# Seven half-size products for eight in the second batch's first feed-forward matmuls

## Chip, cores and metric

One NeuronCore of a Trainium2 chip. The metric is the device time of one execution in microseconds (us), the median of three runs.

## What is computed

Three stages for B = 2 batches of S = 768 tokens, model width 512: attention within clusters (8 heads of 64), then a feed-forward layer with hidden width 2048, then a mixture of 4 experts with hidden width 1024 each. In float32, shortened:

```python
def _moe_ref(x, w_in, w_out):            # x: 1536 x 512
    h = x @ w_in                         # 512 x 2048
    relu6 = np.clip(h + 3.0, 0.0, 6.0)
    g = h * relu6 / 6.0
    return g @ w_out                     # 2048 x 512

def _moe2_ref(x, domain_probs, w1, w2):  # w1: 4 x 512 x 1024
    p = domain_probs / (domain_probs.sum(-1, keepdims=True) + 1e-09)
    out = 0
    for e in range(4):
        h = np.maximum(x @ w1[e], 0.0)
        out += p[:, e:e + 1] * (h @ w2[e])
    return out
```

## The kernel before

**Number format.** Each operand of a matmul stands as a high part (a copy rounded to the matmul's float32 format) and a low part (the rest). A product of two tiles is three matmuls into the same PSUM bank: high by high, high by low, low by high (`mm3`, L784 to L793). For a weight tile of 128x512, `split_w` (L747 to L751) makes the high part on ScalarE (ACT, L749) and the low part on GpSimd (POOL, L750); the latter reads both the raw tile and the high part.

**Stages.** Both batches run attention (`Attn`), then `Moe1` (the feed-forward layer, L797) and `Moe2` (the experts, L846). The attention of batch 1 is planned under `Moe2` of batch 0, so that `Moe1` and `Moe2` of batch 1 come last and alone. The hidden width is cut into chunks c of 512 columns: 4 in `Moe1`, 8 in `Moe2`. The tokens are cut into 2 blocks (blk) of MB = 384. A chunk's weights are 4 tiles k (128 rows each) of w_in or w1 in pool `wi` and 4 of w_out or w2 in pool `wo`. Each pool has 4 places, so that a chunk's weights go into the places of the chunk before.

**First matmul** (`g1`). For each block and each f (4 groups of 128 hidden columns), 12 matmuls of 128x384 (4 tiles k, 3 matmuls each) into one PSUM bank. In `Moe1` then ACT makes t (L820), VectorE (DVE) multiplies t by the bank (L821), ACT copies the high part of g (L822), DVE makes its low part g (L826). In `Moe2` ACT makes the high part of h (L864), DVE the low part (L865).

**Second matmul** (`g2`). In `Moe1` for each block and each of 4 groups d of output columns, 12 matmuls of 128x384, added by DVE to acc (L839; for c = 0 ACT copies, L837). Once c = 3 is added, ACT and DVE make x2h and x2l (L842, L843), the input of `Moe2`. In `Moe2`, for each block and each of 3 groups of 128 tokens, 12 matmuls of 128x512 with h as the stationary operand, scaled and added to oa by DVE (L880; L878 for c = 0), which is stored at the last chunk (L884). g2 of one block is planned among g1 of the next one. `psg`, `psm` in the profile are the PSUM banks of `Moe1` and `Moe2`; the pool `ps_mb` behind them has 3.

**Order.** The whole program is recorded first. `Order.plan` then takes, engine by engine, the instruction that a model of the engines would start earliest; ties go to the lower priority number, which is a planned time (the loop over `seq`). The model's durations are formulas in `act`, `dve`, `pool`, `mm`. Loads of weights all go through SP's queue.

```python
def dve(n, prio, fn, r, w, fast=False, ap=False):
    return add("DVE", 1e-3 * (n / (1.92 if fast else 0.96) + 68 + 60 * ap), prio, fn, r, w)
def pool(n, prio, fn, r, w, ns=2.1):
    return add("POOL", 1e-3 * (n * ns + 150), prio, fn, r, w)
mm = lambda n: 1e-3 * (n / 2.4 + 2.5)
```

Of the kernel before, what the change touches and what calls it, by code (L numbers as in the profile page):

```python
# [99 lines left out]
class Buf:  # L100
    """A tile that its first writer allocates."""
# [230 lines left out]
def body(ctx: ExitStack, tc: tile.TileContext, qk, nat, vd, cent, w_in, w_out, probs, w1, w2, out):  # L332
# [48 lines left out]
    g_ps = o.group("psum", after=(g_pa,), keep=True)  # L381
# [18 lines left out]
    p_pm = [Pool("ps_ma", 1, g_pa, True), Pool("ps_mb", 3, g_ps, True)]  # L400
# [3 lines left out]
    p_acc = [Pool(f"acc{b}", 1, g_m[b]) for b in range(B)]  # L404
# [65 lines left out]
    class Attn:  # L470
# [76 lines left out]
            # scores against the centroids: rows (half of the tokens, head, q or k, centroid)  # L547
# [104 lines left out]
        def block(self, hp, blk, p, kinds, xb, avp):  # L652
            """A block of queries of a pair of heads; p(i) is the priority of its i-th unit."""
# [46 lines left out]
        def scores(self, qa, qb, ka, kb, q0, tb, n, p):  # L700
# [44 lines left out]
    wt, wscr = {}, {}  # L745
# [51 lines left out]
    class Moe1:  # L797
# [7 lines left out]
        def load(self, c, n, p):  # L805
# [40 lines left out]
    class Moe2:  # L846
# [64 lines left out]
    seq = [(st, c, blk) for st in stages for c in range(st.nch) for blk in range(NMB)]  # L911
# [4 lines left out]
    for st, c, blk in seq:  # L916
# [3 lines left out]
        tail = [(prev, d) for d in range(prev[0].n2)] if prev else []  # L920
# [6 lines left out]

        cut = len(tail) - 1 if blk == 0 else 0
# [83 lines left out]
```

## Time and profile before

| | |
|---|---|
| median of 3 runs | 1090.08 us (1089.95 to 1092.23) |
| span of the profiled execution, first to last instruction | 1088.1 us |
| PE (TensorE) matmul busy | 995.6 us, 91% |
| DVE / ACT / POOL busy | 634.4 / 478.7 / 497.8 us |
| granted TensorE clock, mean | 0.965 |
| PE in 850 to 1050 us | 50.00 of every 50 us |
| DVE in the same stretches | 13.25 to 13.64 of 50 us |

The profiled execution's own time is known as its span; the runs' times hold what lies around it too. The page's slices show the program in three parts: up to some 300 us attention and the conversion of weights for batch 0 with the other engines as busy as PE, then `Moe2` of batch 0 with the attention of batch 1, and from some 680 us on the two feed-forward stages of batch 1. Matmul spans overlap (a matmul of 0.33 us starts 0.17 us after the one before), so the cost of a matmul is read from starts, not from spans.

### The profile page before, as it was taken

What the parts mean: (1) busy time and instruction counts of PE and PEld (TensorE: products, weight loads), DVE (VectorE), ACT (ScalarE), POOL (GpSimd) and SP (SyncE); (2) the same over time, 40 slices, a digit from 0 to 9 for tenths busy, and PEclk for the clock granted to TensorE, in tenths of its full rate; (3) what the DMA queues carried; (4) which work ended last, traced back from release to release, by engine and by line L of the source; (5) the groups of instructions that cost most, each with busy time, mean ns of one, the idle gap of its engine ahead of it and who ended that gap; (6) DMA issues with size and microseconds to landing.
All of it is one profiled execution on the core that took longest, in us unless ns stands there. A gap on an engine that the chain in (4) does not pass through costs nothing.

```text
span 1088.1 us, 15473 instructions
## 1 busy us (share of the span) xinstructions
PE 995.6 (91%) x5699; PEld 898.5 (83%) x5699; DVE 634.4 (58%) x1103; ACT 478.7 (44%) x893; POOL 497.8 (46%) x385
## 2 busy tenths in 40 slices
PE   3666677988999999999999999999999999999998
PEld 1555556887898888888898898999999899999997
DVE  8999995999536785576476475334453222222222
ACT  6667774545255554345345343444342232222220
POOL 3576864546346776356256164234332333132330
PEclk9678888999999999999999999999999999999999
DMA  8599799676006486367266176222121221112211
GB/s 259 128 201 184 140 187 242 223 245 200 30 2 208 125 168 148 94 134 162 80 145 137 44 156 155 77 78 79 41 67 48 78 78 64 53 50 69 78 39 58
DMA packets 192363, 129.32 MB, mean 119 GB/s; under 512 B 155488, under 2 KB 155488, under 8 KB 192288
## 3 DMA queue, kind: packets, MB, share of 16 engines
q1 hardware_dynamic: 192288, 128.34, 46.1%
q8 instruction: 44, 0.72, 0.3%
q14 instruction: 31, 0.25, 0.1%
HBM read 74.51 MB, written 11.53 MB: 79 GB/s over the span
## 4 chain that ended last, share of the span: by engine, by line
PE 45%; DVE 18%; issue 16%; DMA 9%; POOL 8%; ACT 3%; SPq 1%; POOLq 0%; ACTq 0%; DVEq 0%
PE psm L789 12%; PE psm L791 12%; PE psm L790 12%; DMA pt<-p 6%; POOL w L750 4%; DVE p L741 4%; DVE ut L717 2%; PE psg L790 2%; DVE wconv L773 2%; DVE wconv L770 2%; PE psv L686 2%; PE psg L789 2%; PE psg L791 2%; DVE wconv L775 1%; POOL p L734 1%
## 5 line engine op out<-in xcount | busy, mean ns | idle before, releaser
L750 POOL TENSOR_TENSOR w<-wraw,w 128x512 fp32r<-128x512 f32 x160 | 213.6, 1365 | 289.7 <-ACT w L749 283.6
L864 ACT ACTIVATE h<-psm 128x384 fp32r<-128x384 f32 x128 | 62.4, 488 | 254.9 <-PE psm L791 252.1
L789 PE MATMUL psm<-x2h,w 128*128 128x384 f32 x512 | 173.2, 338 | 0.0
L791 PE MATMUL psm<-x2h,w 128*128 128x384 f32 x512 | 171.8, 336 | 0.0
L790 PE MATMUL psm<-x2l,w 128*128 128x384 f32 x512 | 171.5, 335 | 0.0
L865 DVE SCALAR_TENSOR_TENSOR h<-psm,h 128x384 fp32r<-128x384 f32 x128 | 71.0, 555 | 144.9 <-ACT h L864 144.7
L789 PE MATMUL psm<-w,h 128*128 128x512 f32 x384 | 151.5, 395 | 0.4 <-DVE h L865 0.4
L791 PE MATMUL psm<-w,h 128*128 128x512 f32 x384 | 150.8, 393 | 0.0
L790 PE MATMUL psm<-w,h 128*128 128x512 f32 x384 | 150.4, 392 | 0.0
L880 DVE SCALAR_TENSOR_TENSOR oa<-psm,pr,oa 128x512 f32<-128x512 f32 x84 | 62.8, 748 | 100.8 <-PE psm L791 100.8
L718 ACT ACTIVATE e<-pss,ut 128x768 f32<-128x768 f32 x96 | 86.0, 897 | 72.4 <-DVE ut L717 50.3
L789 PEld LDWEIGHTS psm<-x2h,w 128*128 128x128 f32 x512 | 96.1, 188 | 4.1 <-issue 2.4
L749 ACT ACTIVATE w<-wraw 128x512 fp32r<-128x512 f32 x160 | 93.7, 624 | 11.8 <-PE psm L791 8.1
L741 DVE SCALAR_TENSOR_TENSOR p<-e,ut,p 128x768 f16<-128x768 f32 x62 | 87.6, 1420 | 17.5 <-POOL p L739 15.7
L790 PEld LDWEIGHTS psm<-x2l,w 128*128 128x128 f32 x512 | 96.2, 188 | 1.3
L791 PEld LDWEIGHTS psm<-x2h,w 128*128 128x128 f32 x512 | 96.1, 188 | 0.0
L790 PE MATMUL psg<-g,w 128*128 128x384 f32 x256 | 88.9, 347 | 6.2 <-DVE g L826 4.4
L789 PE MATMUL psg<-x1h,w 128*128 128x384 f32 x256 | 87.3, 341 | 7.7 <-DVE t L821 7.6
L717 DVE TENSOR_REDUCE ut<-pss 128x1 f32<-128x768 f32 x96 | 90.0, 944 | 4.6 <-PE pss L712 4.5
L789 PE MATMUL psg<-g,w 128*128 128x384 f32 x256 | 87.9, 343 | 4.9 <-DVE t L821 4.5
L791 PE MATMUL psg<-g,w 128*128 128x384 f32 x256 | 87.4, 341 | 0.3 <-POOL w L750 0.3
L791 PE MATMUL psg<-x1h,w 128*128 128x384 f32 x256 | 86.7, 339 | 0.0
(125 smaller groups left out, 1913.4 us busy)
## 6 DMA issues: line engine op xcount, KB each, us to landing
wraw<-in_w SPq DMA_DIRECT2D x128, 256.0 KB, 3.2
r<-in_w_in SPq DMA_DIRECT2D x16, 512.0 KB, 5.0
r<-in_w_out SPq DMA_DIRECT2D x16, 512.0 KB, 4.4
nat<-in_nat SPq DMA_DIRECT2D x16, 384.0 KB, 4.4
raw<-in_qk SPq DMA_DIRECT2D x16, 384.0 KB, 4.2
scr_i<-wconv SPq DMA_DIRECT2D x16, 256.0 KB, 2.4
scr_o<-wconv SPq DMA_DIRECT2D x16, 256.0 KB, 3.2
wraw<-scr_i SPq DMA_DIRECT2D x16, 256.0 KB, 2.6
```

The lines of the kernel that those rows point to most:

```text
L686: nc.tensor.matmul(ps[64 * q:64 * q + 64], vs[vi][:, q, t], pts[q][:, :, pi * NT + t], start=i == 0, stop=i == n - 1)
L717: dve(S, p, lambda: nc.vector.tensor_reduce(out=nb(), in_=ps[:, :, 0:HS], axis=AX.XY, op=ALU.max, negate=True), [ps], [(tb, n)])
L718: act(S, p, lambda: nc.scalar.activation(out=e.t.rearrange("p (a b) -> p a b", a=2), in_=ps[:, :, 0:HS], func=AF.Exp, bias=nb(), scale=1.0 ...
L741: dve(S, p, lambda: nc.vector.scalar_tensor_tensor(out=pp[:, j, 1], in0=e.t, scalar=rs(), in1=pp[:, j, 0], op0=ALU.mult, op1=ALU.subtract) ...
L749: act(512, p, lambda: nc.scalar.activation(out=w[:, 0], in_=raw.t, func=AF.Copy), [raw], [(w, 0)])
L750: pool(512, p, lambda: nc.gpsimd.tensor_tensor(out=w[:, 1], in0=raw.t, in1=w[:, 0].bitcast(F32), op=ALU.subtract), [raw, (w, 0)], [(w, 1)])
L789: nc.tensor.matmul(o_, ah, bh, start=i == 0, stop=False)
L790: nc.tensor.matmul(o_, ah, bl, start=False, stop=False)
L791: nc.tensor.matmul(o_, al, bh, start=False, stop=i == 3)
L864: act(MB, p, lambda: nc.scalar.activation(out=h[:, 0], in_=ps[:, 0:MB], func=AF.Relu), [ps], [(h, 0)], ps=True)
L865: dve(MB, p, lambda: nc.vector.scalar_tensor_tensor(out=h[:, 1], in0=ps[:, 0:MB], scalar=0.0, in1=h[:, 0].bitcast(F32), op0=ALU.max, op1=A ...
L880: dve(512, p, lambda: nc.vector.scalar_tensor_tensor(out=oa[:, t], in0=ps.t, scalar=q, in1=oa[:, t], op0=ALU.mult, op1=ALU.add), [ps, pr], ...
```

## The change

For batch 1, in every chunk but c = 0 of each stage, the first matmul is computed as a whole: W (512 x 512) and X (512 x 768) are cut into quarters (two row halves of 256, two column halves), and the product's four quarters come from 7 products of quarters or sums of quarters instead of 8 (Strassen's identity, in Winograd's form).

- `sums_x`, once a stage: four sums of quarters of x (tiles tx0 to tx3, high and low). In `Moe1` they are built from x1h and x1l (28 DVE instructions of 128x384 and 8 ACT ones), in `Moe2` in place in acc (16 and 8).
- `load_w(..., sums=True)`: after the split of the raw weight tiles, four sums of quarters in place in the raw tiles (8 DVE instructions of 128x256), then their high parts on ACT (4) and low parts on DVE (4 of 128x512), into tiles ws.
- `g1w`, for each half i of the columns: 7 products of 6 matmuls each, every one into a bank of the new pool `ps_w` (5 banks). An ACT copy (u1) and 7 DVE adds put them together, partly in PSUM, partly in SBUF tiles "keep". `post` is what followed the matmuls in `g1`.
- Memory: `ps_w` opens when the attention's banks close; acc of batch 1 takes the place of oa; block 1's g and h get a pool `gw` of 5.
- Plan: both blocks of such a chunk are one step; the second matmuls of the chunk before are placed ahead of it and between the products of the second half.

The core of the diff (line numbers of the new kernel differ from those above; removed comments are left out):

```diff
-    p_acc = [Pool(f"acc{b}", 1, g_m[b]) for b in range(B)]
+    p_acc = [Pool("acc0", 1, g_m[0]), p_oa]
+    p_w = Pool("ps_w", 5, g_pf, True)
+    p_tx = Pool("tx", 8, g_m[1])
+    p_ws = Pool("ws", 8, g_m[1])
+    p_tmp = Pool("tmp", 6, g_m[1])
+    p_gw = Pool("gw", 5, g_m[1])
...
+        for k in range(2 if sums else 0):
+            u, v = raws[k], raws[k + 2]
+            a11, a21, a12, a22 = (lambda x=x, h=h: x[:, 256 * h:256 * h + 256] for x in (u, v) for h in range(2))
+            for o_, x, y, op, rd, w in ((a22, a21, a22, ALU.add, u, v), (a21, a11, a21, ALU.subtract, u, u), (a11, a22, a11, ALU.subtract, v, u), (a12, a12, a11, ALU.subtract, u, v)):
+                dve(256, p, lambda o_=o_, x=x, y=y, op=op: nc.vector.tensor_tensor(out=o_(), in0=x(), in1=y(), op=op), [rd] if rd is not w else [], [w])
+            for x in (u, v):
+                w = Buf(p_ws, [128, 2, 512], F32R, "ws")
+                act(512, p, lambda w=w, x=x: nc.scalar.activation(out=w[:, 0], in_=x.t, func=AF.Copy), [x], [(w, 0)])
...
+                    dve(512, p, lambda lo=lo: lo(nc.vector), [x, (w, 0)], [(w, 1)])
...
+            n = {1: (a(0, 0), bq(0, 0)), 2: (a(1, 0), bq(1, 0)), 3: (sm(2), bq(1, 1)), 4: (a(1, 1), tq(3)),
+                 5: (sm(3), tq(0)), 6: (sm(0), tq(1)), 7: (sm(1), tq(2))}
...
+            def kept(ps, k, j):
+                o = Buf(p_tmp, [128, MB], F32, "keep")
+                if k is None:
+                    act(MB, ts[j], lambda: nc.scalar.activation(out=o.t, in_=ps[:, 0:MB], func=AF.Copy), [ps], [o], ps=True)
+                else:
+                    dve(MB, ts[j], lambda: nc.vector.tensor_tensor(out=o.t, in0=ps[:, 0:MB], in1=k.t, op=ALU.add), [ps, k], [o])
+                return o
+
+            def done(blk, f, ps, k, j):
+                dve(MB, ts[j], lambda: nc.vector.tensor_tensor(out=ps[:, 0:MB], in0=ps[:, 0:MB], in1=k.t, op=ALU.add), [k], [ps])
+                self.post(c, blk, f, ps, lambda: ps[:, 0:MB], ts[j])
+
+            u1 = kept(prod(1), None, 1)
+            done(0, i, prod(2), u1, 2)
+            u2 = kept(prod(6), u1, 6)
+            u3 = kept(prod(7), u2, 7)
+            done(0, i + 2, prod(4), u3, 4)
+            p5 = prod(5)
+            o5 = kept(p5, u2, 5)
+            o4 = kept(p5, u3, 5)
+            self.post(c, 1, i + 2, o4, lambda: o4.t, ts[5])
+            done(1, i, prod(3), o5, 3)
...
+        wino = lambda self, c: self.b == 1 and c > 0
...
+            cut = len(tail) // 2 if prev[0].wino(prev[1]) else len(tail) - 1
+            t = second(tail[:cut], t)
+            for i in range(2):
+                ts = {}
+                for n, j in enumerate((1, 2, 6, 7, 4, 5, 3)):
+                    if i == 1 and n in (0, 2, 4):
+                        t = second(tail[cut + n // 2:cut + n // 2 + 1], t)
+                    ts[j] = t
+                    t += G3
+                if i == 1:
+                    t = second(tail[cut + 3:], t)
+                todo[st].append((st.g1w, (c, i, ts)))
```

**How the order moves.** DVE in `Moe1` of batch 1, around the first matmul of chunk 1. Before, t and the low half of g of one group after another (t, g: tiles of `post`; psg1: PSUM bank of a first product):

```order
L821 SCALAR_TENSOR_TENSOR t_7445<-t_7445,psg1_7427 128x384
L826 TENSOR_TENSOR g_7462<-t_7445,g_7462 128x384
L821 SCALAR_TENSOR_TENSOR t_7493<-t_7493,psg1_7464 128x384
L826 TENSOR_TENSOR g_7505<-t_7493,g_7505 128x384
L821 SCALAR_TENSOR_TENSOR t_7515<-t_7515,psg1_7487 128x384
L826 TENSOR_TENSOR g_7526<-t_7515,g_7526 128x384
```

With the change, the end of the same chunk's second half (psw: bank of a product; keep: a kept sum; wraw: raw tiles of the next chunk's w_in; ws: their sums' parts):

```order
L946 SCALAR_TENSOR_TENSOR t_7706<-t_7706,psw_7671 128x384
L775 TENSOR_TENSOR wraw_7570<-wraw_7570 128x256
L896 TENSOR_TENSOR keep_7726<-psw_7681,keep_7688 128x384
L775 TENSOR_TENSOR wraw_7570<-wraw_7610,wraw_7570 128x256
L775 TENSOR_TENSOR wraw_7633<-wraw_7595,wraw_7633 128x256
L775 TENSOR_TENSOR wraw_7610<-wraw_7610,wraw_7570 128x256
L775 TENSOR_TENSOR wraw_7595<-wraw_7595 128x256
L779 TENSOR_TENSOR ws_7742<-wraw_7570,ws_7742 128x512
L779 TENSOR_TENSOR ws_7750<-wraw_7610,ws_7750 128x512
L775 TENSOR_TENSOR wraw_7595<-wraw_7633,wraw_7595 128x256
L951 TENSOR_TENSOR g_7724<-t_7706,g_7724 128x384
```

Between t_7706 and its low half g_7724, which a second matmul reads, stand nine instructions, eight of them for the next chunk's weights.

PE between two chunks of `Moe1` of batch 1. Before, at the end of chunk 1's second matmuls (psg2: bank of a second product; w_7481 is w_out's last tile of chunk 1, w_7654 w_in's first of chunk 2):

```order
L789 MATMUL psg2_7745<-g_7693,w_7481 128x384
L790 MATMUL psg2_7745<-g_7693,w_7481 128x384
L791 MATMUL psg2_7745<-g_7693,w_7481 128x384
L789 MATMUL psg1_7768<-x1h1_4182,w_7654 128x384
L790 MATMUL psg1_7768<-x1l1_4188,w_7654 128x384
L791 MATMUL psg1_7768<-x1h1_4182,w_7654 128x384
```

With the change, at chunk 1's last second product (w_7584: w_out's last tile of chunk 1, w_8019: its first of chunk 2):

```order
L814 MATMUL psg2_8007<-g_7794,w_7584 128x384
L815 MATMUL psg2_8007<-g_7794,w_7584 128x384
L816 MATMUL psg2_8007<-g_7794,w_7584 128x384
L814 MATMUL psg2_8037<-g_7859,w_8019 128x384
L815 MATMUL psg2_8037<-g_7859,w_8019 128x384
L816 MATMUL psg2_8037<-g_7859,w_8019 128x384
```

The first products that stood between the second products of two chunks are gone from there; chunk 2's second product follows chunk 1's at once.

## Rows read from the trace of the kernel before

**Rows 1.** Busy time by stretch, all engines: 250 to 300 us, Moe1 chunks, one Moe2 chunk.
```profile
core 0: us, PE busy (x) PEld busy (x) DVE busy (x) ACT busy (x) POOL busy (x), PEclk, DMA share, GB/s
250.00:300.00 50.00, 43.37 (x229) 40.45 (x228) 36.36 (x53) 17.61 (x33) 23.75 (x18) 0.97 0.28 93
707.00:741.00 34.00, 33.54 (x193) 33.12 (x192) 12.92 (x20) 14.57 (x29) 10.93 (x9) 1.00 0.22 63
775.00:809.00 34.00, 33.54 (x194) 33.12 (x193) 18.09 (x28) 14.79 (x29) 11.04 (x8) 1.00 0.20 63
809.00:843.00 34.00, 33.54 (x182) 31.68 (x182) 13.90 (x22) 11.27 (x24) 11.04 (x8) 1.00 0.20 62
909.00:942.00 33.00, 33.00 (x169) 30.07 (x168) 8.80 (x15) 8.39 (x17) 10.11 (x8) 1.00 0.20 64
```

**Rows 2.** Timeline of PE: matmul starts in Moe1, then Moe2 (start us, us, what).
```profile
701.74 0.33 PE L789 MATMUL psg<-x1h,w 128*128 128x384 f32 x1
...
707.29 0.33 PE L791 MATMUL psg<-x1h,w 128*128 128x384 f32 x1
...
884.41 0.39 PE L789 MATMUL psm<-w,h 128*128 128x512 f32 x1
...
887.17 0.33 PE L789 MATMUL psm<-x2h,w 128*128 128x384 f32 x1
...
895.52 0.39 PE L789 MATMUL psm<-w,h 128*128 128x512 f32 x1
```

**Rows 3.** Waits, 690 to 1088 us: total us, times, longest.
```profile
PE psg L790 <- DVE g L826: 1.8, 4, 0.5
```

**Rows 4.** Groups by line, 700 to 1088 us (busy us, mean ns, idle before).
```profile
L750 POOL TENSOR_TENSOR w<-wraw,w 128x512 fp32r<-128x512 f32 x88 | 114.9, 1340 | 254.7 <-ACT w L749 254.7
...
L865 DVE SCALAR_TENSOR_TENSOR h<-psm,h 128x384 fp32r<-128x384 f32 x64 | 35.7, 558 | 103.9 <-ACT h L864 103.9
L880 DVE SCALAR_TENSOR_TENSOR oa<-psm,pr,oa 128x512 f32<-128x512 f32 x42 | 31.5, 751 | 76.7 <-PE psm L791 76.7
L826 DVE TENSOR_TENSOR g<-t,g 128x384 fp32r<-128x384 f32 x27 | 24.3, 901 | 17.2 <-ACT g L822 17.2
...
L821 DVE SCALAR_TENSOR_TENSOR t<-t,psg 128x384 f32<-128x384 f32 x27 | 14.9, 551 | 31.3 <-ACT t L820 31.3
...
L839 DVE TENSOR_TENSOR acc<-acc,psg 128x384 f32<-128x384 f32 x24 | 13.2, 553 | 17.9 <-PE psg L791 17.9
```

**Rows 5.** Groups by line of VectorE, whole execution.
```profile
L449 DVE TENSOR_TENSOR cw<-cn 128x64 f32<-128x64 f32 x1 | 0.2, 225 | 0.2 <-DMA cn<-in_cent 0.2
```

**Rows 6.** The line of g's low half: min/median/max ns.
```profile
L826 DVE TENSOR_TENSOR g<-t,g x40: 544/559/1692, 193.2 to 812.0; 128x384 fp32r<-128x384 f32 x40
```

**Rows 7.** Timelines of ScalarE, GpSimd and VectorE at a reload of w2.
```profile
918.51 2.70 ACT L749 ACTIVATE w<-wraw 128x512 fp32r<-128x512 f32 x4 [0.26 <-PE psm L791]
...
919.22 5.05 POOL L750 TENSOR_TENSOR w<-wraw,w 128x512 fp32r<-128x512 f32 x4 [4.79 <-ACT w L749]
...
920.53 0.75 DVE L880 SCALAR_TENSOR_TENSOR oa<-psm,pr,oa 128x512 f32<-128x512 f32 x1 [1.68 <-PE psm L791]
```

**Rows 8.** Timeline of VectorE, then of GpSimd, around a split of weights.
```profile
708.49 0.54 DVE L821 SCALAR_TENSOR_TENSOR t<-t,psg 128x384 f32<-128x384 f32 x1
709.79 1.59 DVE L826 TENSOR_TENSOR g<-t,g 128x384 fp32r<-128x384 f32 x1 [0.76 <-ACT g L822]
...
706.86 5.66 POOL L750 TENSOR_TENSOR w<-wraw,w 128x512 fp32r<-128x512 f32 x4 [19.54 <-ACT w L749]
```

**Rows 9.** Timeline of VectorE: last x1l, and t of chunk 0's second block.
```profile
683.68 0.48 DVE L696 SCALAR_TENSOR_TENSOR x1l<-psv,sv,x1h 128x256 fp32r<-128x256 f32 x1 [0.89 <-ACT x1h L694]
...
704.17 0.55 DVE L821 SCALAR_TENSOR_TENSOR t<-t,psg 128x384 f32<-128x384 f32 x1 [8.70 <-ACT t L820]
```

**Rows 10.** DMA issues (KB each, us to landing), whole execution.
```profile
wraw<-in_w SPq DMA_DIRECT2D x128, 256.0 KB, 3.2
```

**Rows 11.** The page's first line.
```profile
span 1088.1 us, 15473 instructions
```

More of the change, by code (lines that the diff above doesn't have):

```diff
@@ L380, in body @@
     g_pa = o.group("psum")
-    g_ps = o.group("psum", after=(g_pa,), keep=True)
+    g_pm = o.group("psum", after=(g_pa,), keep=True)
+    g_ps = o.group("psum", after=(g_pa,))
+    g_pf = o.group("psum", after=(g_ps,), keep=True)
     g_m[0] = o.group("left", after=(g_a[0], g_l0))
@@ L751, in split_w, with load_w @@
         wt.setdefault(key, []).append(w)
-    def load_w(key, src, p):
+    def load_w(key, src, p, sums=False):
+        raws = []
         for k in range(4):
@@ L798, in body @@
+    class Moe1(Wino):
         names, nch, n2 = "io", NC1, 4
@@ L809, in load @@
             else:
-                load_w(key, lambda k: wscr[key[1:]][k], p)
+                load_w(key, lambda k: wscr[key[1:]][k], p, sums=n == "i" and self.wino(c))
+        wino = lambda self, c: self.b == 1 and c > 0
+        src = lambda self: list(x1[1])
+        xs = lambda self: x1[1]
         def g1(self, c, blk, f, p):
@@ L817, in g1, with post @@
                 lambda k: [ps, w[k]] + xkeys(b, k, blk), xkeys(b, KD - 1, blk) if (b, c, blk) == (0, 0, 0) else ())
+            self.post(c, blk, f, ps, lambda: ps[:, 0:MB], p)
+        def post(self, c, blk, f, ps, out, p):
+            b, sb = self.b, ps.pool is p_tmp
             t = Buf(p_t[b], [128, MB], F32, "t")
-            g = Buf(p_g, [128, 2, MB], F32R, "g")
-            act(MB, p, lambda: nc.scalar.activation(out=t.t, in_=ps[:, 0:MB], func=AF.Relu, scale=1.0 / 6.0, bias=half[:, 0:1]), [ps], [t], ps=True, ap=True)
-            dve(MB, p, lambda: nc.vector.scalar_tensor_tensor(out=t.t, in0=t.t, scalar=1.0, in1=ps[:, 0:MB], op0=ALU.min, op1=ALU.mult), [ps], [t])
+            g = Buf(p_gw if self.wino(c) and blk else p_g, [128, 2, MB], F32R, "g")
+            act(MB, p, lambda: nc.scalar.activation(out=t.t, in_=out(), func=AF.Relu, scale=1.0 / 6.0, bias=half[:, 0:1]), [ps], [t], ps=True, ap=True)
+            dve(MB, p, lambda: nc.vector.scalar_tensor_tensor(out=t.t, in0=t.t, scalar=1.0, in1=out(), op0=ALU.min, op1=ALU.mult), [ps], [t])
             act(MB, p, lambda: nc.scalar.activation(out=g[:, 0], in_=t.t, func=AF.Copy), [t], [(g, 0)])
@@ L854, in load @@
             src = {"1": w1, "2": w2}[n][c]
-            load_w((self.b, n, c), lambda k: src[:, k], p)
+            load_w((self.b, n, c), lambda k: src[:, k], p, sums=n == "1" and self.wino(c))
+        wino = lambda self, c: self.b == 1 and c > 0
+        src = lambda self: [stages[2].acc]
+        xs = lambda self: x2s[1]
         def g1(self, c, blk, f, p):
@@ L910, in body @@
         stages += [Moe1(b), Moe2(b)]
-    seq = [(st, c, blk) for st in stages for c in range(st.nch) for blk in range(NMB)]
+    seq = [(st, c, blk) for st in stages for c in range(st.nch) for blk in range(NMB) if not (st.wino(c) and blk)]
     prev = None
@@ L919, in body @@
         start.setdefault(st, t)
-        tail = [(prev, d) for d in range(prev[0].n2)] if prev else []
+        tail = [(prev[:2] + (k,), d) for k in ((0, 1) if prev[0].wino(prev[1]) else prev[2:]) for d in range(prev[0].n2)] if prev else []
         def second(x, t):
@@ L926, in second @@
             return t
+        if st.wino(c):
+            if c == 1:
+                todo[st].append((st.sums_x, (start[st] + G["wx"],)))
+            todo[st].append((st.load, (c, st.names[0], t - G["wl"])))
+            G3 = 1.04
+            cut = len(tail) // 2 if prev[0].wino(prev[1]) else len(tail) - 1
[10 more added lines that the diff above has]
+                todo[st].append((st.g1w, (c, i, ts)))
+                if i == 0:
+                    todo[st].append((st.load, (c, st.names[1], t - G["wl"])))
+            prev = (st, c, 0)
+            continue
         cut = len(tail) - 1 if blk == 0 else 0
@@ L941, in body @@
         prev = (st, c, blk)
-    for d in range(prev[0].n2):
-        todo[prev[0]].append((prev[0].g2, (*prev[1:], d, t)))
-        t += G2
+    for k in range(NMB) if prev[0].wino(prev[1]) else prev[2:]:
+        for d in range(prev[0].n2):
+            todo[prev[0]].append((prev[0].g2, (*prev[:2], k, d, t)[1:]))
+            t += G2
     def trace(st):
```

77 lines of the change are left out of this document (70 added, 7 removed).

## The prediction

> **What bounds the kernel now.** I read the views in this order: the busy times by stretch, to find what is full where the change works; the matmul starts, for the price of a matmul; the groups by line, for the price of everything else; the timelines of VectorE, GpSimd and ScalarE, for what collides. The first 4459 PE instructions (all of batch 0 and of the second batch's attention) stand in the same order in both programs, so only what follows the first chunk of the second batch's first feed-forward stage counts, about 690 us onward. There TensorE is full: 33.54 of 34 us in each of the four windows from 707 to 843, about a chunk each of the first stage (Moe1), and 33.00 of 33 in a chunk of the second (Moe2), at a granted clock of 1.00, the 2.4 GHz level [rows 1]. VectorE is at 12.92 to 18.09 us per chunk in Moe1 and only 8.80 in Moe2. So a matmul taken away is time taken away, as long as VectorE can carry what it is given for it. In Moe1 it has 16 us free in a chunk, in Moe2 24.
>
> **Removed.** A chunk's first matmul is 8 products of 12 matmuls; the change makes 14 half-size products of 6. That is 84 for 96, in 3 chunks of Moe1 and 7 of Moe2: 120 fewer, and PE's list is shorter by just these 120, so the change does what it says. Matmuls of 384 columns start 5.55 us apart over 32 steps in Moe1 and 8.35 us over 48 in Moe2 [rows 2]: 0.1735 us each. **-20.8 us**, 2.08 per chunk. The waits of today, 0.46 us in each of the four windows (the waits view gives 1.8 us of matmuls to the low half of g), stand at places that are rebuilt: **-1.8** [rows 1, 3].
>
> **Added on VectorE, per chunk.** 14 adds of a product in PSUM to a kept sum, 128x384: like the acc add, 0.553 us, 7.7 us [rows 4]. For the weights, 8 sums of 128x256 and 4 low halves of 128x512, both operands in SBUF. No row has these shapes with two SBUF operands: 128x64 takes 0.225 [rows 5] and 128x384 0.559 when undisturbed [rows 6]. A line through both gives 0.42 and 0.69, so 6.1 us; the bounds are 0.225 and 0.559 for the first and 0.559 and 0.75 (the 128x512 oa update [rows 4]) for the second, 4.0 to 7.5 us. Together 13.8 us per chunk. ScalarE's 2 copies and 4 halves fit: four w passes of 128x512 last 2.70 [rows 7], so these six stay under 4.1 us, and it has 19 us free [rows 1]. GpSimd's list does not change at all.
>
> **What that makes of a chunk.** Moe2: 8 h at 0.558, 6 oa at 0.751 and 13.8 make 22.8 us of VectorE in 33.0 - 2.1 = 30.9 us of TensorE. It fits, with 8 us to spare. Moe1: 8 t, 8 g and 8 acc at 0.55 to 0.56 make 13.3, with 13.8 some 27.1 of 31.2. That fits only if nothing disturbs it, and something does: the low half of g, which reads two SBUF operands, takes 0.56 us undisturbed [rows 6] but 1.59 us inside a GpSimd split of weights, while the t update beside it, with one operand in PSUM, stays at 0.54 [rows 8]. Of the 27 such g in this stretch 14 were hit; at 24.3 us in all they cost 9.3 us more than 27 times 0.556, **0.66 us per hit** [rows 4]. Moe1 goes from 8 such instructions per chunk to 20. The Trainium skill, "SBUF — State Buffer", section "Who interferes with whom", states this rule: a VectorE instruction with two SBUF inputs contends with a GpSimd one that reads SBUF, and the earlier holds the port for its whole length. The trace agrees, and the rule speaks against this change, whose 12 weight sums per chunk are of that kind while GpSimd still makes 8 splits. By it, adds out of PSUM stay clean.
>
> **Where TensorE will wait.** I walk the two orders against each other.
> - *Moe1, chunk 0:* 28 sums and low halves of x join VectorE's queue between the last x1l (683.68) and the t at 704.17 [rows 9], with 9 old ones: 37 times 0.556 is 20.6 us in 20.5. They fit, nearly: **+1.0** (0 to 3).
> - *Moe1, chunk 1:* its 14 products stand without second matmuls between them. From the sum of product 2 to the low half g that the next second matmuls need, VectorE has 35 instructions: 25 of 128x384 (13.9 us), 7 of 128x256 (2.9) and 3 of 128x512 (2.1), 18.9; four hits by GpSimd add 2.6 and a wait for ScalarE 0.6: 22.1 us. TensorE in that time has 105 matmuls, 18.2 us. **+3.9** (0.7 without hits, 7 with eight).
> - *Reload of w_out in Moe1:* before, four first products (8.3 us) stood between the last second matmul of one chunk and the first of the next, which has other weights in the same four tiles. Now the two touch, from chunk 1 to 2 and from 2 to 3. Each tile must be released, copied and split. In Moe2 the first split starts at 919.22 and takes 1.27, so it is ready at 920.5, when the chunk's last product is just being read [rows 7]. That tile was free three quarters of a product before the end, 2.07 us where 12 matmuls of 512 columns last 2.76 [rows 2], but only 1.56 in Moe1, where they last 2.08: it is ready 0.5 us later, and with semaphores some 0.8 us is bare. **+1.6** (0.8 to 4).
> - *Moe1, chunks 2 and 3:* 27.1 us plus 20 two-SBUF instructions of which half are hit at 0.66 would be 33.7 against 31.2; but part of the sums fall after the splits. **+3.0** (0 to 6).
> - *Moe2, chunk 0:* sums of x and the first oa write, which must wait for acc (they now share memory). VectorE finishes both a product before TensorE needs its bank: **+1.0** (0 to 3).
> - *Moe2, reloads of w2:* two quarter products, then three products, cover the four splits of 5.06 us [rows 7]; only the first tile is late by 0.2, six times: **+1.2** (0 to 2.4).
>
> SP's list keeps its order but for one store of batch 0, which comes one load later. The raw tiles of w1, though, land only as the splits of w2 free their places: the second at 1.5 us after the reload begins, plus 3.2 to land [rows 10], 0.7 for the copy and 1.3 for the split, 6.7 us. In front of it TensorE has three second products and three first ones, 11 us, so I count it at nothing; without that cover it would be up to 3 us a chunk. The end of the program is the same last product, oa update and store.
>
> **Sum.** -20.8 - 1.8 + 1.0 + 3.9 + 1.6 + 3.0 + 1.0 + 1.2 = -10.9 us. The profiled execution's span is 1088.1 [rows 11]; the median time of the runs, 1090.08, lies 2.0 above it, and I keep these 2.0 for what lies around the span. 1088.1 - 10.9 + 2.0 = **1079.2 us**.
>
> **Rivals.**
> 1. *VectorE keeps up* (chance 0.18). If it finds its idle time between the hits, only the reloads and one us at each stage's start stay, some 4: 1090.1 - 22.6 + 4 = 1071.5. For it speaks Moe2 (70% of the gain, 8 us spare); against it the 27.1 of 31.2 in Moe1.
> 2. *GpSimd's splits bind VectorE* (0.14), slower. With w us lost for each of 8 splits, VectorE needs 27.1 + 8w in a Moe1 chunk and 22.8 + 8w in Moe2, against 31.2 and 30.9. At w = 1.2, nearly a whole split of 1.27, that is 5.5 too much three times and 1.5 too much seven times: 27, with the 4.8 us of the other waits 32 against 22.6, **1099.5**. It decides from w = 1.07. The g of 1.59 [rows 8] speaks for it, the mean of 0.66 on half the instructions against it. By the rule quoted above, an instruction that comes while the other runs loses all the rest of it, which is half a split on average, 0.65: not enough.
> 3. *PSUM banks* (0.16): five banks for 1.04 us products, each held through an add, a ScalarE pass and another VectorE pass. If VectorE, bunched with the weight sums, runs late by one product and a half in every Moe2 chunk, 7 times 1.5 is 10.5: 1089.7, no change. Against it: for seven products in a row (7.3 us) VectorE has 11 instructions, 6.1 us.
>
> If TensorE waits, its clock may follow: the stretch of 250 to 300, with 43.4 of 50 us busy, had 0.97 [rows 1]. Over 100 us of Moe1 that is 3 us, and it is in the range.
>
> **Chances and range.** My case (1074 to 1086) 0.52, rival 1 0.18, rival 2 0.14, rival 3 0.16, of whose part three quarters lie within 0.2% (2.2 us, about what a measurement of this kernel can tell from no change) and the rest is faster. So faster 0.74, same 0.12, slower 0.14. The range 1072 to 1090.5 takes in my bounds, most of rival 1 and all of rival 3; it leaves out about 0.05 below and 0.14 above.
>
> **What would show it.** PE matmuls 120 fewer, still 0.1735 apart. VectorE near 30 us in a Moe1 chunk and 23 in a Moe2 chunk. TensorE's idle time almost all before 850 us, put down to the low half g, to the sums of the weights and, at the chunks' ends, to GpSimd's w. The weight sums at 0.42 and 0.69 or over 1 us when hit. I am wrong if Moe2 chunks are longer than 31.5 us, if the adds out of PSUM cost more than 0.6, or if Moe1 chunks 2 and 3 lose more than 3 us each or nothing.

## The result, and the profile after

The changed kernel takes **1076.86 us** (median of 4 runs, 1076.05 to 1078.58) against 1090.01 (4 runs, 1088.86 to 1092.23): a ratio of 0.9878, 95% interval 0.9863 to 0.9893, 1.2% faster. The page's first lines of the changed kernel:

```profile
span 1075.5 us, 15704 instructions
...
PE 984.3 (92%) x5579; PEld 882.6 (82%) x5579; DVE 787.9 (73%) x1407; ACT 516.3 (48%) x969; POOL 499.7 (46%) x385
```

TensorE has 120 matmuls less, VectorE 304 instructions and 153 us of busy time more; GpSimd's work is the same.

**A common starting point.** Up to the end of the second batch's attention both programs run the same list, yet even that part differs by up to some 4 us from run to run. Its last instructions on TensorE are 36 small matmuls of the attention (psv). TensorE isn't waiting there, though a text on record below calls the place a "2.18-us wait". The first matmul behind them is the same instruction in every kernel here; the timeline of PE, before and after:

```profile
683.06 0.50 PE L789 MATMUL psm<-w,h 128*128 128x512 f32 x1
...
681.04 0.50 PE L814 MATMUL psm<-w,h 128*128 128x512 f32 x1
```

So 2.0 of the 12.6 us between the two spans come from a part that the change doesn't touch. **From that point to the end** it is 405.0 us before and 394.5 after: the change gives 10.6 us. I use this second number (the "tail") beside the medians below. It is free of what the common part does, but it comes from one profiled execution of each kernel.

Busy time by stretch after, Moe1 from chunk 0's second half (706), then its chunks, the passage to Moe2 (802 to 836), a stretch of Moe2, then the ten us in which TensorE waits longest and two us behind that wait; the columns of [rows 1]:

```profile
706.00:737.00 31.00, 29.83 (x170) 29.19 (x169) 27.77 (x51) 20.50 (x41) 15.90 (x12) 1.00 0.27 77
737.00:769.00 32.00, 31.79 (x180) 31.00 (x178) 25.18 (x46) 14.66 (x28) 7.66 (x6) 1.00 0.19 56
769.00:802.00 33.00, 32.37 (x181) 31.33 (x180) 28.18 (x52) 15.32 (x29) 11.45 (x9) 1.00 0.21 66
802.00:836.00 34.00, 30.08 (x152) 28.53 (x153) 25.45 (x39) 13.08 (x27) 9.67 (x7) 0.95 0.20 64
900.00:1000.00 100.00, 99.91 (x494) 89.16 (x493) 71.78 (x127) 37.32 (x70) 34.59 (x27) 1.00 0.20 65
...
820.00:830.00 10.00, 6.46 (x27) 5.94 (x26) 6.84 (x10) 3.21 (x8) 2.63 (x2) 0.83 0.17 53
826.00:828.00 2.00, 2.00 (x8) 2.00 (x8) 0.32 (x1) 0.00 (x0) 0.00 (x0) 0.50 0.00 0
```

VectorE went from 13 to 18 us in a Moe1 chunk to 25 to 28, and TensorE is still full in Moe2. What it loses lies in Moe1 and, most of all, between 820 and 830. The waits of TensorE from 684 us on (us in total, times, longest; before there was one line, [rows 3]):

```profile
PE psm L814 <- DVE h L997: 3.5, 1, 3.5
PE psg L815 <- DVE g L951: 1.2, 2, 0.6
PE psg L814 <- DVE acc L964: 0.8, 2, 0.4
PE psg L816 <- POOL w L758: 0.4, 2, 0.2
```

The longest, on the timeline of PE:

```profile
821.19 0.34 PE L816 MATMUL psm<-x2h,w 128*128 128x384 f32 x1
825.06 0.41 PE L814 MATMUL psm<-x2h,w 128*128 128x384 f32 x1 [3.54 <-DVE h L997]
...
826.07 0.52 PE L815 MATMUL psm<-x2l,w 128*128 128x384 f32 x1
826.39 0.52 PE L816 MATMUL psm<-x2h,w 128*128 128x384 f32 x1
```

TensorE stops ahead of the fifth first product of Moe2's chunk 0: it needs one of three banks, that of the second one, which its h must release (L997). It starts 3.70 us late, and then its matmuls start 0.32 us apart instead of 0.1735: the granted clock is 0.50 there, the 1.2 GHz level, after 3.5 us without work. Up to 829.0 that costs another 1.65 us. Why h is late stands in VectorE's queue, with GpSimd's below:

```profile
814.79 0.55 DVE L997 SCALAR_TENSOR_TENSOR h<-psm,h 128x384 fp32r<-128x384 f32 x1
815.26 1.25 DVE L835 TENSOR_TENSOR acc<-acc 128x384 f32<-128x384 f32 x1
816.43 1.64 DVE L840 TENSOR_TENSOR tx<-acc,tx 128x384 fp32r<-128x384 f32 x1
...
819.86 1.65 DVE L968 TENSOR_TENSOR x2l<-acc,x2h 128x384 fp32r<-128x384 f32 x1
821.54 1.50 DVE L835 TENSOR_TENSOR acc<-acc 128x384 f32<-128x384 f32 x1
...
824.37 0.54 DVE L997 SCALAR_TENSOR_TENSOR h<-psm,h 128x384 fp32r<-128x384 f32 x1
...
814.79 2.87 POOL L758 TENSOR_TENSOR w<-wraw,w 128x512 fp32r<-128x512 f32 x2 [8.44 <-ACT w L757]
819.69 2.94 POOL L758 TENSOR_TENSOR w<-wraw,w 128x512 fp32r<-128x512 f32 x2 [2.04 <-ACT w L757]
```

Four instructions with two SBUF operands (the new sums of x, and x2l) lie beside the four splits of chunk 0's w2 and take 1.25 to 1.65 us instead of 0.56. Between the two h stand eleven instructions, nine of them those sums.

Last, the timeline of VectorE in Moe1's chunk 1:

```profile
722.45 0.55 DVE L896 TENSOR_TENSOR keep<-psw,keep 128x384 f32<-128x384 f32 x1
722.92 0.56 DVE L900 TENSOR_TENSOR psw<-psw,keep 128x384 f32<-128x384 f32 x1
723.38 0.55 DVE L951 TENSOR_TENSOR g<-t,g 128x384 fp32r<-128x384 f32 x1
...
728.85 1.32 DVE L951 TENSOR_TENSOR g<-t,g 128x384 fp32r<-128x384 f32 x1
...
730.56 1.04 DVE L775 TENSOR_TENSOR wraw<-wraw 128x256 f32<-128x256 f32 x1
...
732.79 1.42 DVE L775 TENSOR_TENSOR wraw<-wraw 128x256 f32<-128x256 f32 x4
734.14 1.29 DVE L779 TENSOR_TENSOR ws<-wraw,ws 128x512 fp32r<-128x512 f32 x2
735.35 0.42 DVE L775 TENSOR_TENSOR wraw<-wraw 128x256 f32<-128x256 f32 x1
```

Look at the starts. The first instructions, of 0.55 us, stand **0.47 us** apart: the next one starts before the last has ended. Two low halves of 128x512 last 1.29 together, so 0.60 each and not 0.68; four sums of 128x256 last 1.42, so 0.34 each and not 0.42.

### The profile page after: what moved, and what is told of

Same layout as the page of the kernel before. It is cut to its first block, busy times and chain, and to the rows that moved or that the text cites. A ratio compares the mean times of both kernels' runs of the same rounds, so it can differ in the third digit from the quotient of the medians.

```text
span 1075.5 us, 15704 instructions
## 1 busy us (share of the span) xinstructions
PE 984.3 (92%) x5579; PEld 882.6 (82%) x5579; DVE 787.9 (73%) x1407; ACT 516.3 (48%) x969; POOL 499.7 (46%) x385
## 4 chain that ended last, share of the span: by engine, by line
PE 40%; DVE 19%; DMA 11%; issue 10%; POOL 6%; ACT 3%; SPq 0%; POOLq 0%; DVEq 0%; ACTq 0%
PE psm L814 7%; PE psm L815 7%; PE psm L816 7%; DMA pt<-p 6%; PE psg L815 3%; PE psg L816 3%; PE psg L814 3%; DVE p L749 3%; PE psw L886 3%; PE psw L884 3%; PE psw L885 3%; POOL w L758 2%; DMA wraw<-in_w 1%; DVE g L951 1%; DVE wconv L798 1%
## 5 line engine op out<-in xcount | busy, mean ns | idle before, releaser
L758 POOL TENSOR_TENSOR w<-wraw,w 128x512 fp32r<-128x512 f32 x160 | 216.6, 1378 | 286.4 <-ACT w L757 279.8
L814 PE MATMUL psm<-x2h,w 128*128 128x384 f32 x288 | 98.8, 343 | 3.5 <-DVE h L997 3.5
L749 DVE SCALAR_TENSOR_TENSOR p<-e,ut,p 128x768 f16<-128x768 f32 x62 | 87.5, 1418 | 19.0 <-POOL p L747 15.8
L816 PE MATMUL psm<-x2h,w 128*128 128x384 f32 x288 | 97.5, 338 | 0.0
L815 PE MATMUL psm<-x2l,w 128*128 128x384 f32 x288 | 97.1, 337 | 0.0
L814 PEld LDWEIGHTS psm<-w,h 128*128 128x128 f32 x384 | 72.3, 188 | 16.5 <-issue 1.8
L816 PEld LDWEIGHTS psm<-w,h 128*128 128x128 f32 x384 | 72.1, 188 | 15.9 <-DVE h L997 0.2
L815 PEld LDWEIGHTS psm<-w,h 128*128 128x128 f32 x384 | 72.3, 188 | 14.6 <-POOL w L758 1.8
L997 DVE SCALAR_TENSOR_TENSOR h<-psm,h 128x384 fp32r<-128x384 f32 x72 | 39.6, 552 | 49.7 <-ACT h L996 49.5
L996 ACT ACTIVATE h<-psm 128x384 fp32r<-128x384 f32 x72 | 34.8, 485 | 82.1 <-PE psm L816 79.5
L747 POOL TENSOR_SCALAR p<-e,ut 128x768 f16<-128x768 f32 x49 | 47.0, 959 | 54.4 <-DMA pt<-p 23.9
L718 PE MATMUL pss<-ka,qa 128*128 128x384 f32 x192 | 66.0, 429 | 0.5 <-ACT e L726 0.5
```

What stands on the lines that cost most here:

```text
L718: nc.tensor.matmul(ps[:, f, 0:HS], qa[:, qs], ka[:, f * HS:f * HS + HS], start=True, stop=False)
L747: pool(S, p, lambda: nc.gpsimd.tensor_scalar(out=pp[:, j, 0], in0=e.t, scalar1=rs(), scalar2=1.0, op0=ALU.mult, op1=ALU.mult), [e, key], [ ...
L749: dve(S, p, lambda: nc.vector.scalar_tensor_tensor(out=pp[:, j, 1], in0=e.t, scalar=rs(), in1=pp[:, j, 0], op0=ALU.mult, op1=ALU.subtract) ...
L758: pool(512, p, lambda: nc.gpsimd.tensor_tensor(out=w[:, 1], in0=raw.t, in1=w[:, 0].bitcast(F32), op=ALU.subtract), [raw, (w, 0)], [(w, 1)])
L814: nc.tensor.matmul(o_, ah, bh, start=i == 0, stop=False)
L815: nc.tensor.matmul(o_, ah, bl, start=False, stop=False)
```

## Experiments

### One stage alone

```diff
 # e1_moe2_only: Moe1, e2_moe1_only: Moe2
-        wino = lambda self, c: self.b == 1 and c > 0
+        wino = lambda self, c: False
```

> The seven products in the second stage alone; the first stage's chunks are as before. Theory (the gain is 0.1735 us per matmul taken away, and what is lost again is lost at a few named places: 5.4 us in the second stage's chunk 0, some 2 us spread over its other chunks, 5.5 us in the first stage): 84 matmuls fewer, -14.6; lost 5.4 to 7.4 us in the second stage; so 7 to 9 us under the kernel before, 1081 to 1083. Rival (the loss belongs to a VectorE that is overloaded all over the last 400 us and follows its load): with 3 chunks less on VectorE, nearly no loss, 1075 to 1077.

> The seven products in the first stage alone; the second stage's chunks are as before, so neither its sums of x nor its chunk 0 are changed. Theory: 36 matmuls fewer, -6.2; the waits of before on the low half of g, -3.1, go; 5 to 6 us of new waits stay (the first second matmuls of chunk 1, two reloads of w_out): 3 to 5 us under the kernel before, 1085 to 1087. Rival (a first stage whose VectorE needs 27.1 of 31.2 us gains nothing, and all of the gain is the second stage's): no change, 1089 to 1091.

**Measured.** Moe2 alone: 1077.22 us (1076.9 to 1080.21), ratio 0.9892 (0.9874 to 0.9909), tail 393.8, a gain of **11.2**. Moe1 alone: 1086.13 (1083.86 to 1087.65), ratio 0.9964 (0.995 to 0.9977), tail 401.0, a gain of **4.0**. Together 15.2, where both at once give 10.6. (The medians, each against the kernel before in the same session, say 12.2 and 3.3 against 13.2 for both: the same sign, a smaller difference, with the common part in it.) For Moe1 alone the time is the theory's. For Moe2 alone the theory falls: 3.4 us of its 14.6 are lost and not 5.4 to 7.4, and the time lies just above the rival's range. In the first kernel the wait for h in Moe2's chunk 0 is small, by its waits view,

```profile
PE psm L814 <- DVE h L997: 0.7, 1, 0.7
```

though the same splits fall as one burst and hit VectorE too, by the timelines of GpSimd and VectorE:

```profile
821.82 6.25 POOL L758 TENSOR_TENSOR w<-wraw,w 128x512 fp32r<-128x512 f32 x4 [5.51 <-ACT w L757]
...
824.16 2.76 DVE L835 TENSOR_TENSOR acc<-acc 128x384 f32<-128x384 f32 x2
```

In the second, Moe1's waits are those of the changed kernel and nothing waits after 803. So the 4.7 us between 15.2 and 10.6 belong to neither stage: they are the place where the two meet, the 3.70 us of wait and the matmuls at half clock. What differs there is the order: in e1 the splits cost VectorE as much between the two h (3.9 us against 3.8), but only seven instructions stand between them and not eleven. The order was not changed by itself in any run.

### The wait in Moe2's chunk 0, from two sides

```diff
 # e3_memset, in split_w
+        if key == (1, "2", 0):
+            pool(512, p, lambda: nc.gpsimd.memset(w[:, 1].bitcast(F32), 0.0), [raw, (w, 0)], [(w, 1)])
+        else: # as before
 # e4_banks, in Moe2.g1
-            ps = Buf(p_m, [128, 512], F32, "psm1", "moe")
+            ps = Buf(p_w if (self.b, c) == (1, 0) else p_m, [128, 512], F32, "psm1", "moe" if (self.b, c) != (1, 0) else "")
```

> The low halves of the four w2 tiles of the second batch's expert chunk 0 are not computed: GpSimd fills them with zeros (four instructions that write SBUF and read nothing) in the place of its four splits; the order of all engines is unchanged. Theory (the 3.7 us for which TensorE waits in the second stage's chunk 0 are the 3.9 us that four two-operand VectorE instructions lose to GpSimd's splits, and the clock that falls behind it costs 1.7 more): those four take 0.56 us each, the wait falls under 1 us, the clock stays at 1.00, 4 to 5.4 us under the changed kernel, 1071.5 to 1073. Rival (the 24 added VectorE instructions of the sums of x are the load, with or without hits; or the ScalarE passes they wait for): the wait stays over 2.5 us, 1075.5 to 1077.

> The first products of the second stage's chunk 0 go into the five PSUM banks that the seven products use later, in place of the three shared with the second matmuls; the order of all engines is unchanged. Theory (TensorE stands in chunk 0 because its third bank waits for an h that is late behind the sums of x; VectorE catches up within 4 us): with more banks TensorE goes on, the wait falls under 1 us and the clock stays up, 4 to 5.4 us under the changed kernel, 1071.5 to 1073. Rival (what is late is h itself, which the second products read next): the wait only moves to the second products' h, 1075 to 1077.

**Measured.** e3: 1073.07 us (1071.16 to 1074.39), ratio 0.9847 (0.9828 to 0.9866), tail 388.9. e4: 1073.81 (1073.16 to 1075.09), ratio 0.9856 (0.9841 to 0.987), tail 389.8. Both medians lie above the range expected (1071.5 to 1073), e4's by 0.8; by the tail the gains over the changed kernel are 5.5 and 4.7 us. Both rivals fall all the same. In e3, the timeline of VectorE at the same place of the order, and of GpSimd:

```profile
818.84 0.55 DVE L971 TENSOR_TENSOR x2l<-acc,x2h 128x384 fp32r<-128x384 f32 x1
819.42 0.56 DVE L838 TENSOR_TENSOR acc<-acc 128x384 f32<-128x384 f32 x1
...
814.60 2.11 POOL L759 MEMSET w<- 128x512 f32 x4 [7.48 <-PE psg L819]
```

The sums are back at 0.56, h comes in time, and the wait is gone. In e4 the splits still hit VectorE (1.25, 1.65, 1.65 and 1.53 us) and h is as late as it was, but TensorE has five banks instead of three and goes on; 0.3 us of wait is left. The granted clock is 1.00 from 802 to 836 in both. So in this order the wait needs both: VectorE held up by the splits, and the three banks running out. The gain of e4's tail, 15.3, is just what the single stages add up to.

### What is left: the reloads of w_out

```diff
 # e5_cover: e4, and in the loop over seq
+            at = (0, 1, 2, 4) if len(tail) == 8 else (0, 2, 4)
...
-                    if i == 1 and n in (0, 2, 4):
-                        t = second(tail[cut + n // 2:cut + n // 2 + 1], t)
+                    if i == 1 and n in at:
+                        t = second(tail[cut + at.index(n):cut + at.index(n) + 1], t)
...
-                    t = second(tail[cut + 3:], t)
+                    t = second(tail[cut + len(at):], t)
```

> The kernel of e4, in which moreover, in Moe1's chunks 2 and 3, the four second products of block 1 stand at places 0, 1, 2 and 4 of the second half instead of 0, 2, 4 and at the end, so that three first products (3.1 us of matmuls) stand between a chunk's last second product and the next chunk's first, which uses the same four tiles of w_out. Theory: the waits at the boundaries from chunk 1 to 2 and from 2 to 3 (0.38 and 0.57 us each in the changed kernel, 1.9 us in all) are the reload of w_out. Chunk 1 still ends as it did, so the boundary from 1 to 2 keeps some of its second products close, and the one from 2 to 3, with its 0.95 us, goes: e4's 1073.8 less 0.5 to 1.9, so 1072 to 1073.3. Rival: the low half of g of block 0, which that last second product had covered by 2.1 us, comes too late instead, and the time stays at 1073.5 or rises to 1077; the wait line of PE then names VectorE's low half of g and not GpSimd's w.

**Measured.** 1070.22 us (1069.48 to 1070.84), ratio 0.9825 (0.9806 to 0.9844), tail 385.8, 3.9 less than e4. That is better than expected: both boundaries are rid of their waits (the edit moves the second products of chunk 1 too, which the text on record denied), and so are other small gaps of TensorE between 760 and 840. One line of TensorE's is left in the waits view after 684 us:

```profile
PE psg L815 <- DVE g L951: 1.1, 2, 0.6
```

The rival, a low half of g that comes too late there, did not show. This kernel does all the work and is faster than the kernel before and the changed one.

### Do GpSimd's splits or VectorE's load set the rest?

```diff
 # e6_nosplit: e4, e8_longset: e5; in split_w, for batch 1
-        pool(512, p, lambda: nc.gpsimd.tensor_tensor(out=w[:, 1], in0=raw.t, in1=w[:, 0].bitcast(F32), op=ALU.subtract), [raw, (w, 0)], [(w, 1)])
+        pool(512, p, lambda: nc.gpsimd.memset(w[:, 1].bitcast(F32), 0.0), [raw, (w, 0)], [(w, 1)])    # e8: three times
 # e7_double: e4, and in load_w
-                    dve(512, p, lambda lo=lo: lo(nc.vector), [x, (w, 0)], [(w, 1)])
+                    for _ in range(2 if key[1] == "i" else 1):
+                        dve(512, p, lambda lo=lo: lo(nc.vector), [x, (w, 0)], [(w, 1)])
```

> The kernel of e4, in which GpSimd fills the low halves of all weights of batch 1 (88 tiles) with zeros instead of subtracting: same engine, same place in the same order, but it reads nothing, and it takes 0.53 us instead of 1.36. It leaves out the low halves of batch 1's weights. Theory: what remains of TensorE's waits behind the second batch's start, some 2 us in Moe1's chunk 1, 1.9 at the two reloads of w_out and 3 in Moe2, comes from GpSimd's splits: by their length (reloads) or by the VectorE instructions that they hold up. With both gone, 3 to 5 us less than e4: 1069 to 1071, and no VectorE instruction of two SBUF operands over 0.75 us. Rival: VectorE's own load sets the waits, and the splits are covered: 1072.5 to 1074.5, VectorE's instructions shorter all the same.

> The kernel of e5, in which GpSimd writes zeros three times over each low half of batch 1's weights instead of subtracting: one memset took 0.53 us in e6, so three take some 1.58, longer than a split's 1.36, but still nothing is read. It leaves out the low halves of batch 1's weights. The order on the other engines is that of e5. Theory: what is left of TensorE's waits in e5, 1.4 us before the second matmuls at 731 and 737 us and small ones in Moe2, is VectorE held up by GpSimd's reads of SBUF; with no reads it goes, whatever GpSimd's length: 383 to 385 us from the resume after the 2.18-us wait to the end (e5 385.8, e6 383.2), a median of 1066 to 1068.5, VectorE's two-SBUF instructions at 0.56, 0.42 and 0.69 us. Rival: it is the splits' length, which holds back the tiles and the raw weights: as e5 or a little slower, 385.5 to 388 from that point, 1070 to 1072.

> The kernel of e4, in which VectorE makes the low halves of Moe1's weight sums twice (12 instructions of 128x512 more, 4 in each of chunks 1 to 3; the second writes the same values). Theory: back to back such an instruction costs 0.60 us, its distance from the next start, and a Moe1 chunk has VectorE busy for 25 to 28 us of 32 to 33, so that 2.4 us more a chunk still fit: 0 to 2.5 us slower than e4, 1073.8 to 1076.3. Rival, the pricing by spans of the prediction, by which chunk 1 is 3.9 us over and chunks 2 and 3 are 1.5 over each: 0.69 each, 2.8 us more in every one of the three chunks, 6 to 8.5 us slower: 1080 to 1082.

**e6, e8 measured.** e6: 1066.64 us (1065.66 to 1067.77), ratio 0.9793 (0.9773 to 0.9813), tail 383.3. e8: 1066.86 (1066.68 to 1067.59), ratio 0.9797 (0.9778 to 0.9816), tail 383.3. In both the waits view of TensorE after 684 us is empty. By the tail e6 is 6.5 us under e4, more than expected; by the median 7.2. e8 is where its theory put it, and its rival falls. The groups by line, 690 us to the end, first of the changed kernel, then of e8:

```profile
L896 DVE TENSOR_TENSOR keep<-psw,keep 128x384 f32<-128x384 f32 x80 | 44.2, 554 | 16.0 <-PE psw L886 15.2
L775 DVE TENSOR_TENSOR wraw<-wraw 128x256 f32<-128x256 f32 x80 | 40.2, 537 | 2.1 <-POOL w L758 1.5
L779 DVE TENSOR_TENSOR ws<-wraw,ws 128x512 fp32r<-128x512 f32 x40 | 26.1, 683 | 0.0
L951 DVE TENSOR_TENSOR g<-t,g 128x384 fp32r<-128x384 f32 x30 | 22.9, 768 | 5.3 <-ACT g L947 5.0
...
L997 DVE SCALAR_TENSOR_TENSOR h<-keep,h 128x384 fp32r<-128x384 f32 x14 | 10.4, 744 | 1.9 <-ACT h L996 1.1
```

```profile
L902 DVE TENSOR_TENSOR keep<-psw,keep 128x384 f32<-128x384 f32 x80 | 44.3, 555 | 20.0 <-PE psw L892 19.6
L781 DVE TENSOR_TENSOR wraw<-wraw 128x256 f32<-128x256 f32 x80 | 30.7, 418 | 0.4
L785 DVE TENSOR_TENSOR ws<-wraw,ws 128x512 fp32r<-128x512 f32 x40 | 26.2, 686 | 0.9 <-ACT ws L784 0.9
L957 DVE TENSOR_TENSOR g<-t,g 128x384 fp32r<-128x384 f32 x30 | 16.4, 552 | 3.8 <-ACT g L953 3.8
...
L1003 DVE SCALAR_TENSOR_TENSOR h<-keep,h 128x384 fp32r<-128x384 f32 x14 | 7.8, 558 | 1.9 <-ACT h L1002 1.1
```

And e8's timeline of GpSimd, its first four tiles after 700 us:

```profile
704.70 6.61 POOL L761 MEMSET w<- 128x512 f32 x12 [18.70 <-PE psg L822]
```

GpSimd is busy for 6.61 us over four tiles in e8, longer than the 5.72 of four splits in the changed kernel, and yet every two-SBUF instruction of VectorE is at its undisturbed price. So it is what a split reads beside VectorE, not how long it holds a tile, that makes the waits which e5 still has. For the reloads of w_out e8 says nothing, since e5 covers them already, and e6 changed the reads and the length at once. Adds out of PSUM (L896) never minded. The Trainium skill, "SBUF — State Buffer", section "Who interferes with whom", says the same of a GpSimd instruction that only writes SBUF: it doesn't contend with two SBUF inputs on VectorE. The trace agrees.

**e7 measured.** 1078.36 us (1076 to 1079.55), ratio 0.9897 (0.987 to 0.9923), tail 394.6: 4.6 us slower than e4 by the median, 4.9 by the tail, between theory and rival. A chunk's sums are made while the chunk before it runs (714 to 720, 738 to 745 and 782 to 788 us). With two of the three doublings, 4.8 us of work, between 714 and 745, TensorE's waits there go from 1.4 to 6.1 us; the last of them, on the timelines of VectorE and PE:

```profile
744.09 0.68 DVE L779 TENSOR_TENSOR ws<-wraw,ws 128x512 fp32r<-128x512 f32 x1
...
745.16 1.01 DVE L965 TENSOR_TENSOR acc<-acc,psg 128x384 f32<-128x384 f32 x2
...
745.76 0.44 PE L815 MATMUL psg<-g,w 128*128 128x384 f32 x1 [1.88 <-DVE acc L965]
```

The third doubling, in chunk 2, brings one new wait of 1.85 us, and 1.0 us at the next boundary goes. So up to the end of chunk 1 VectorE is at its limit, with the splits' hits, and each us more costs one: there the theory is wrong. In chunk 2, for which the pricing by spans had it 1.5 us over, 2.4 us more of work cost 0.9, so it has some room. No doubling falls into chunk 3, which this run doesn't test. The plan also moves a few products here, so the split between the chunks is not exact.

### A later place for the weight sums

```diff
 # e9_lead3: e5, in PAR
-    wsl="DD", wx=4.0, wxs=0.7, wl=6.0,
+    wsl="DD", wx=4.0, wxs=0.7, wl=3.0,
```

> The kernel of e5 with the planned lead of the weights' loads and sums ahead of their chunk cut from 6 us to 3: the plan then puts chunk 2's weight sums later among VectorE's work in Moe1's chunk 1, so that low halves of g stand earlier, and a pair of products changes place. Nothing else changes. Theory: chunk 1's 1.4 us of waits for the low half of g (0.66 and 0.75 us) shrink to under 0.5 and nothing new is late, since the products that need the sums come 10 us later: 1068.5 to 1070.2, no kernel so far faster that keeps all of the work. Rival: VectorE has no spare time in chunk 1 (two doublings of 0.6 us there cost e7 more than their own length), so what it does later waits elsewhere, on the sums: 1070 to 1073.

**Measured.** 1069.73 us (1068.13 to 1070.76), ratio 0.982 (0.9802 to 0.9838), tail 385.8: the same as e5. The theory falls, though the median lies in its range: chunk 1's waits are 0.86 and 0.54 instead of 0.66 and 0.75. The weight sums did move back, but low halves of g then stood in the burst of splits in their stead (timeline of VectorE):

```profile
727.04 3.09 DVE L951 TENSOR_TENSOR g<-t,g 128x384 fp32r<-128x384 f32 x2
```

Two of 0.56 take 3.09 there; in e5 a pair of them took 1.62. In all, the two kernels lose the same 2 us to that burst: in e5 another low half of g and a weight sum were hit too. The waits view puts the longer wait down to ScalarE's high half of g, which waits, through t, for an add of VectorE's that stands behind those two:

```profile
PE psg L814 <- ACT g L947: 0.7, 1, 0.7
PE psg L815 <- DVE g L951: 0.3, 1, 0.3
```

## Why the prediction was right, and which of its terms were not

The forecast was 1079.2 us with 1072 to 1090.5; 1076.86 is in it, and "faster" is the outcome that it gave a chance of 0.74. The sum of the terms, -10.9, is the tail's 10.6; the other 2 us came from the part that both programs share. But the sum is right by luck, because errors cancel: the losses in Moe1 were put nearly 5 us too high and those in Moe2 over 5 us too low.

| term | forecast | measured (starts of PE) |
|---|---|---|
| 120 matmuls at 0.1735 us | -20.8 | -20.8: e6, without waits, gains 21.8 by the tail, old waits included |
| waits of before gone | -1.8 | -2.5 (four of 0.62) |
| Moe1 chunk 0 | +1.0 | 0.3 |
| Moe1 chunk 1 | +3.9 | 1.5 (twice 0.75) |
| reloads of w_out | +1.6 | 1.9 (twice 0.38 and 0.56), and 0.8 in gaps of 0.1 beside them |
| Moe1 chunks 2, 3 | +3.0 | 0.2, no wait of their own |
| Moe2 chunk 0 | +1.0 (0 to 3) | **5.4** (3.70 and 1.65) |
| reloads of w2 | +1.2 | 0.3 in one wait, and 2.1 in gaps too small to be named: a chunk takes 31.39 us (before 33.16), 1.77 less and not 2.08 |

- **Removed work and dropped waits**: right. With no wait left, e6's tail gives the whole of it: 20.8 for the matmuls and 2.5 for the old waits, less some 1.5 in gaps too small to be named.
- **Step that failed: VectorE's price.** The prediction took spans (0.556, 0.42, 0.69) where instructions stand back to back. By starts the 35 instructions of chunk 1 are 25 times 0.467, 7 times 0.335 and 3 times 0.60, 15.8 us instead of 18.9; with the forecast's 2.6 for hits and 0.6 for ScalarE 19.0 against TensorE's 18.2. That gives 0.8, where 1.5 was measured; the other 0.7 stays unexplained. Without hits, in e6 and e8, nothing is left to wait for in chunk 1: by starts 16.4 us with ScalarE's 0.6, which fit into 18.2, where the spans would make it 19.5. A Moe1 chunk is 22.8 us instead of 27.1. The formula `dve` of the kernel's own plan had these prices, n/0.96 + 68 ns: 0.468, 0.335 and 0.601 us. One of the prediction's own signs of being wrong came true as well: chunks 2 and 3 of Moe1 lose nearly nothing of their own. The matmuls had been priced by starts, VectorE was not.
- **Step that failed: Moe2's chunk 0.** "VectorE finishes both a product before TensorE needs its bank" counted no hits there, though the rule on two SBUF operands had been told for Moe1. Four hits (0.7 to 1.1 us each) and only three banks made 3.70, and the clock, which the prediction had put on Moe1, another 1.65. e3 takes all of this away, e4 all but 0.4 us.
- **A term left out**: the 20 instructions per Moe1 chunk with two SBUF operands are 22. Two of the t in Moe1, and two of the h in Moe2, now read a kept sum in SBUF and not a PSUM bank. Against e8 these t take 2.2 and these h 2.6 us more; one t took 1.65 us in the burst ahead of the boundary from chunk 1 to 2.
- **The reloads of w_out**: right in size. e5 shows that place and cover are the cause, but the waits view names acc's bank (0.8) before w (0.4): acc too is held up during that burst of splits, behind three low halves of g and that t.
- **Rival 1** (VectorE keeps up, 1071.5) is what e4 and e5 nearly are, 1073.8 and 1070.2: VectorE keeps up except in chunk 1 and where the stages meet. **Rival 2** needed 1.07 us lost for each split by its text, 1.09 by its sum. The disturbed groups tell what it is: the wraw sums are 9.5 us longer in the changed kernel than in e8, g 6.5, all groups with two SBUF operands together 26.3, which is 0.3 us for each of the 88 splits; the ws halves, which stand behind the splits, lose nothing. **Rival 3**, too few banks, came not with `ps_w` in every Moe2 chunk but once, in the three old ones.

Still open: the 1.4 us in chunk 1, which only a split that reads nothing removed; a version that does so and keeps the low halves wasn't tried.

## What to carry to other kernels

Price an engine's instructions in a full queue by the distance of their starts, and by their spans only where it idles after each: here the spans made VectorE look one fifth fuller than it was. When an engine is given sums of two SBUF operands, walk every place where a GpSimd burst can lie beside them, the seams between stages above all, and count the PSUM banks that wait behind them there. Two changes that each cost little where they stand can cost 4.7 us more together; e4's one line gave all of it back.

## What the hardware showed that was not expected

The spans of VectorE's instructions overlap: with a successor ready, 128x384 in float32 costs 0.47 us for a span of 0.55, 128x512 0.60 for 0.68, 128x256 0.34 for 0.42, some 0.08 us less each. What a split costs beside VectorE depends on the timing: a pair of low halves of g took 1.62 us in e5 and 3.09 in e9. The rows show how. All 33 instructions that were hit after 690 us in the changed kernel end 0.41 to 0.42 us (384 columns) or 0.28 to 0.29 (256 columns) after the end of a split that they began under. So the split of 819.69 and 2.94, two of them, ends at 822.63, and the acc sum of 821.54 and 1.50 at 823.04. A hit waits out the rest of its split. The clock fell to its lower level after an idle of 3.5 us in Moe2's chunk 0 (0.50 granted from 826 to 828), while in e7, with a wait of 1.88 us and 29.18 of 32 us busy, the stretch kept 1.00:

```profile
737.00:769.00 32.00, 29.18 (x164) 28.23 (x163) 25.65 (x52) 13.54 (x26) 1.69 (x2) 1.00 0.11 34
```
